# Seven half-size products in both MLPs, values kept in PSUM, and queues ordered by a list scheduler

## The chip, the core and the metric

The kernel runs on one core of one Trainium2 chip. Five engines with queues of their own share it: TensorE (PE, with its weight loads PEld), VectorE (DVE), ScalarE (ACT), GpSimd (POOL) and SyncE (SP, which here issues the DMAs). Each queue runs in order, and an instruction that waits for another engine holds up all that stands behind it on its own queue. The metric is the device time of one launch in microseconds (us).

## The reference

A clustered attention (2 batches, 8 heads, 768 tokens, head size 64) gives 1536 tokens of 512 features. Two MLPs (512 to 2048 to 512) follow, the first with a squared ReLU, the second with a hard swish:

```python
def _moe_ref(x, w_in, w_out):
    h = np.maximum(x @ w_in, 0.0)
    return (h * h @ w_out).astype(np.float32)

def _moe2_ref(x, w_in, w_out):
    h = x @ w_in
    relu6 = np.clip(h + 3.0, 0.0, 6.0)
    g = h * relu6 / 6.0
    return (g @ w_out).astype(np.float32)

x = np.ascontiguousarray(attn_out.transpose(0, 2, 1, 3)).reshape(B * S, H * D)
x = _moe_ref(x=x, **moe_kwargs)
return _moe2_ref(x=x, **moe2_kwargs)
```

The MLP weights are 64-bit floats in memory.

## The kernel before

Every operand of a large product is split into a rounded high part and a low rest, and a product is three matmuls (high by high, high by low, low by high) that add up in PSUM. `decode` (L183 to 219) turns 64-bit weights into such a pair: a clamp on POOL (L193), a scaled copy on ACT (L198), three integer steps on DVE (L203, L205, L209), a rounding on ACT (L213) and a subtraction (L215).

The attention comes first, in an order written out by hand in tables (up to L846). Its last instructions are the rounding and subtraction of the last tiles on POOL (`eh`, `el`), the last product `a` (L709), its sum `u` (L723), the transposes `tn` (L750) and the last quarter of the normalised result, `xh` and `xl` (L756 to L761). The first quarter of the first product of the first MLP (`emit_early`, 48 matmuls of 384 columns) already runs inside it.

The MLPs follow from L850. Both have four stages (`fq`), in each of which 512 of the 2048 hidden features are made and used. A stage has chunks of 512 tokens (384 in the very first stage). `mm1` (L892) makes one chunk's hidden features: four PSUM banks `h`, in each 4 x 3 matmuls (`products`, L229), then `gate` (L237) squares or gates them and splits them into `gh` and `gl`. `mm2` (L912) multiplies a chunk by the second weights into four banks `o`, and each bank is added to `acc` (L941, L943, L947). The loop at L993 calls `mm1` of a chunk and then `mm2` of the chunk before, so that PE has other work while `gate` runs. The order on each queue is the order in which the code calls; only the first steps have their decoding placed by hand (`decoding`, L972). `mm1` and `mm2` of a chunk are 48 matmuls each.

Of the kernel before, what the change touches and what calls it, by code (L numbers as in the profile page):

```python
# [16 lines left out]
I32 = mybir.dt.int32  # L17
# [110 lines left out]
MOST = 2.0**16 * (2 - 2.0**-3 - 2.0**-23)  # L128


@with_exitstack
def cluster_attention_mlp_kernel(
# [718 lines left out]
    with ExitStack() as mctx:  # L851
        t_p = mctx.enter_context(tc.tile_pool(name="t", bufs=2, reuse_waits="tile"))
        acc_p = mctx.enter_context(tc.tile_pool(name="acc", bufs=1, reuse_waits="tile"))
        wr_p = mctx.enter_context(tc.tile_pool(name="wr", bufs=2, reuse_waits="tile"))
        wd_p = mctx.enter_context(tc.tile_pool(name="wd", bufs=2, reuse_waits="tile"))
        w_p = mctx.enter_context(tc.tile_pool(name="w", bufs=3, reuse_waits="tile"))
        g_p = mctx.enter_context(tc.tile_pool(name="g", bufs=2, reuse_waits="tile"))
        g3_p = mctx.enter_context(tc.tile_pool(name="g3", bufs=1, reuse_waits="tile"))
        ps_h = mctx.enter_context(tc.tile_pool(name="ps_h", bufs=4, space=PSUM, reuse_waits="tile"))
        ps_o = mctx.enter_context(tc.tile_pool(name="ps_o", bufs=4, space=PSUM, reuse_waits="tile"))  # L860

        wts = {(0, 0, 0): (w_first[:, 0], w_first[:, 1])}
        idx = [1]

        def load_w(m, fq, which):

            src = w_src(m, fq, which)
            if idx[0] % 4 == 0:
                w = w0_p.tile([P, 2, 4, 512], F32R, tag="w0", name="w0")
# [12 lines left out]
        def run(steps, n=None):
            for _ in range(n) if n else iter(int, 1):
                if next(steps, 0) == 0:
                    break

        acc = acc_p.tile([P, 4, NT], F32, name="acc")

        acc1 = acc.rearrange("p d t -> p (d t)").rearrange("p (b n) -> p b n", n=DM)
        G = {(0, 0, 0): early[0]}  # L890

        def mm1(m, fq, c0, n, between=None):  # L892
            wh, wl = wts[m, fq, 0]
            if (m, fq, c0 + n) == (0, 0, NT):
                gh, gl = (g3_p.tile([P, NF, n], F32R, tag=x, name=x) for x in ("gh3", "gl3"))
            else:
                gh = g_p.tile([P, NF, TC], F32R, tag="gh", name="gh")[:, :, :n]
                gl = g_p.tile([P, NF, TC], F32R, tag="gl", name="gl")[:, :, :n]
            for fb in range(NF):
                h = ps_h.tile([P, TC], F32, tag="h", name="h")[:, :n]  # L900
                for d in range(ND):
                    products(h, wh, wl, fb, d, slice(c0, c0 + n))
                if between:
                    between(0)
                r = t_p.tile([P, TC], F32, tag="r", name="r")[:, :n]
                g = t_p.tile([P, TC], F32, tag="g", name="g")[:, :n]
                gate(m, h, r, g, gh[:, fb], gl[:, fb])
                if between:
# [126 lines left out]
```

## Time and profile before

| | before |
|---|---|
| median of 3 runs | 790.9 us (790.01 to 791.15) |
| span of the profiled execution | 789.0 us |
| PE busy | 771.8 us, 98% of the span |
| DVE, ACT, POOL busy | 547.9, 399.7, 328.5 us |
| granted TensorE clock | full in all 40 slices |
| DMA | 67.27 MB, mean 85 GB/s |

The profiled execution took 789.0 us from its first to its last instruction; the median of the timed runs lies 1.9 us above it. In the page, the busy shares say which engine has no room; the slices say where; the chain of work that ended last says which instructions the end waits for; the groups by shape say what one instruction costs. PE is fully busy in each slice after about 300 us, and the chain there has PE alone.

The matmuls outside the attention, counted in the program's order of the kernel before: 2004 of 512 columns, 336 of 384 and 24 of 256.

### The profile page before, as it was taken

How to read it: one execution, taken by the hardware profiler on the slowest of the kernel's cores; microseconds unless marked ns; L12 is line 12 of the kernel's file. 1: busy time of each engine (PE TensorE's matmuls, PEld its weight loads, DVE VectorE, ACT ScalarE, POOL GpSimd, SP SyncE). 2: the span in 40 equal slices, each digit the busy share in tenths (PEclk: the TensorE clock that was granted, in tenths of full speed). 3: DMA queues.
4: the chain of work that ended last, by engine and by line, in shares of the span. 5: the costliest groups of instructions: out<-in, count | busy, mean ns of one | idle time of the engine just before them, and what ended most of it. 6: DMA issues, size and time to landing. Idle time of an engine off the chain costs nothing.

```text
span 789.0 us, 11571 instructions
## 1 busy us (share of the span) xinstructions
PE 771.8 (98%) x4066; PEld 674.8 (86%) x4066; DVE 547.9 (69%) x891; ACT 399.7 (51%) x803; POOL 328.5 (42%) x440
## 2 busy tenths in 40 slices
PE   7999999999999999999999999999999999999998
PEld 6789999999989899988888888888888888888887
DVE  5889999999998588885654748579465585443332
ACT  4899899899887665554333433424334132111110
POOL 1668778778786562332221313334222121111110
PEclk9999999999999999999999999999999999999999
DMA  8847845836510234441311203022031120000012
GB/s 178 177 106 174 181 94 135 175 89 146 131 34 14 81 97 137 143 145 67 108 50 57 84 24 107 22 86 76 31 107 53 54 81 1 0 1 1 23 46 93
DMA packets 58203, 67.27 MB, mean 85 GB/s; under 512 B 41153, under 2 KB 41409, under 8 KB 58145
## 3 DMA queue, kind: packets, MB, share of 16 engines
q1 hardware_dynamic: 58144, 66.54, 31.7%
q8 instruction: 32, 0.52, 0.3%
q14 instruction: 27, 0.21, 0.1%
HBM read 43.02 MB, written 3.15 MB: 59 GB/s over the span
## 4 chain that ended last, share of the span: by engine, by line
PE 85%; ACT 5%; DVE 5%; issue 2%; POOL 2%; DMA 1%; SPq 0%; ACTq 0%; POOLq 0%
PE o L933 33%; PE h L232 29%; PE a L709 6%; PE t L682 6%; PE s L646 3%; PE s L649 3%; ACT e L666 2%; PE tsim L438 2%; PE tq L393 1%; ACT mt L511 1%; DVE nm L655 1%; ACT eh L692 1%; DVE el L693 1%; ACT et L178 1%; ACT tmp L178 1%
## 5 line engine op out<-in xcount | busy, mean ns | idle before, releaser
L232 PE MATMUL h<-xh,w 128*128 128x512 f32 (+1 forms) x800 | 244.8, 381 | 0.0
L232 PEld LDWEIGHTS h<-xh,w 128*128 128x128 f32 x800 | 149.3, 188 | 26.4 <-DVE xx L756 0.2
L181 POOL TENSOR_SCALAR gh<-g 128x512 fp32r<-128x512 f32 (+1 forms) x96 | 68.9, 718 | 228.1 <-DVE g L243 150.0
L232 PE MATMUL h<-xl,w 128*128 128x512 f32 (+1 forms) x400 | 152.2, 380 | 0.0
L933 PE MATMUL o<-w,gh 128*128 128x512 f32 (+1 forms) x392 | 120.5, 385 | 0.0
L245 DVE TENSOR_TENSOR gl<-g,gh 128x512 fp32r<-128x512 f32 (+1 forms) x96 | 70.4, 736 | 70.4 <-POOL gh L181 70.4
L933 PE MATMUL o<-gh,w 128*128 128x512 f32 (+1 forms) x384 | 114.8, 376 | 0.0
L193 POOL TENSOR_SCALAR t<-wr 128x512 f32<-128x512 f32 (+1 forms) x66 | 56.0, 852 | 113.2 <-DVE w L215 44.5
L682 PE MATMUL t<-ident,e 128*128 128x128 f32 x576 | 93.4, 275 | 8.1 <-ACT e L666 7.4
L242 ACT ACTIVATE r<-h,three 128x512 f32<-128x512 f32 x48 | 32.8, 686 | 120.6 <-PE h L232 120.6
L655 DVE TENSOR_REDUCE nm<-s 128x1 f32<-128x768 f32 x96 | 90.7, 946 | 1.2 <-PE s L649 0.3
L682 PEld LDWEIGHTS t<-ident,e 128*128 128x128 f32 x576 | 70.6, 140 | 20.4 <-ACT e L666 11.4
L666 ACT ACTIVATE e<-s,nm 128x768 f32<-128x768 f32 x96 | 86.3, 899 | 2.1 <-DVE nm L655 1.6
L232 PEld LDWEIGHTS h<-xl,w 128*128 128x128 f32 x400 | 75.1, 188 | 13.0
L933 PEld LDWEIGHTS o<-w,gh 128*128 128x128 f32 x392 | 73.1, 188 | 14.8
L690 POOL TENSOR_TENSOR el<-et,eh 128x384 fp32r<-128x384 f32 x80 | 81.8, 1023 | 6.7
L933 PEld LDWEIGHTS o<-gh,w 128*128 128x128 f32 x384 | 71.4, 188 | 11.6 <-issue 0.4
L198 ACT ACTIVATE u<-t 128x512 f32<-128x512 f32 (+1 forms) x68 | 41.3, 607 | 68.4 <-POOL t L193 67.9
L933 PE MATMUL o<-w,gl 128*128 128x512 f32 (+1 forms) x196 | 75.4, 385 | 0.0
L213 ACT ACTIVATE w<-t 128x512 fp32r<-128x512 f32 (+1 forms) x68 | 39.3, 604 | 69.3 <-PE o L933 41.7
L933 PE MATMUL o<-gl,w 128*128 128x512 f32 (+1 forms) x192 | 72.1, 375 | 0.0
L693 DVE TENSOR_TENSOR el<-t,eh 128x384 fp32r<-128x384 f32 x112 | 61.4, 551 | 14.7 <-ACT eh L692 13.3
(118 smaller groups left out, 1288.2 us busy)
## 6 DMA issues: line engine op xcount, KB each, us to landing
wr<-in_moe_w_out_dram SPq DMA_DIRECT2D x32, 512.0 KB, 3.3
op<-HL SPq DMA_DIRECT2D x84, 192.0 KB, 4.4
wr<-in_moe_w_in_dram SPq DMA_DIRECT2D x28, 512.0 KB, 3.7
rawv<-in_v_dram SPq DMA_DIRECT2D x16, 192.0 KB, 3.6
out_dram<-acc SPq DMA_DIRECT2D x11, 256.0 KB, 2.0
rawq<-in_q_dram SPq DMA_DIRECT2D x14, 192.0 KB, 4.5
rawk<-in_k_dram SPq DMA_DIRECT2D x14, 192.0 KB, 4.0
wr<-in_moe_w_in_dram SPq DMA_DIRECT2D x8, 256.0 KB, 3.0
```

Of the source, the lines that this page charges most:

```text
L181: nc.gpsimd.tensor_scalar(dst, src, 1.0, 0.0, op0=ALU.mult, op1=ALU.add)
L193: (nc.vector if clamp_on_dve or not on_dve and E_CLAMP == "v" else nc.gpsimd).tensor_scalar(t, f(hw), MOST, -MOST, op0=ALU.min, op1=ALU.max)
L198: nc.scalar.activation(u, t, AF.Copy, scale=2.0**-112)
L232: nc.tensor.matmul(h, w[:, d, fs], x[:, d, cs], start=(d == 0 and n == 0), stop=(d == ND - 1 and n == 2),)
L245: nc.vector.tensor_sub(gl, g, f(gh))
L655: nc.vector.tensor_reduce(nm, S_t[n][:, :, :HS], axis=AX.XY, op=ALU.max, negate=True)
L666: nc.scalar.activation(e, s[:, :, :HS], AF.Exp, bias=nm, accum_out=sums[u][:, i * R + r : i * R + r + 1])
L682: nc.tensor.transpose(t[:, c, :], E_t[n][:, half, c * P : (c + 1) * P], ident)
L690: nc.gpsimd.tensor_sub(el, et, f(eh))
L693: nc.vector.tensor_sub(el, t, f(eh))
L709: nc.tensor.matmul(a[:, :HS], vs[:, kr, i, :], x[:, kr, :], start=(kr == 0 and x is eh), stop=(kr == R - 1 and x is el),)
L933: nc.tensor.matmul(o, lhsT, rhs, start=(k == 0), stop=(k == 3 * NF - 1))
```

## The change

The attention is untouched. The MLP part is written anew.

**Seven products.** In six of the eight stages (all but the first of each MLP) the first product is no longer 48 matmuls for a chunk. Two token chunks of 384, two halves of the 512 input features and two halves of 256 hidden features form a 2 x 2 by 2 x 2 block product, and `quad` computes it with seven products of halves and sums of halves instead of eight. A product is 6 matmuls of 384 columns, so a quad is 42 matmuls for four results instead of 48. The sums of weights (`weights_in`: four sums on POOL and five halves split anew) are made in each stage, the sums of tokens (`token_sums`) once for each MLP. Partial results are kept (`keep`, a copy on ACT) and added (`plus`, on DVE, in PSUM).

**Widths.** All first products, and the second products of the first MLP, are now 384 columns wide; the second products of the second MLP stay at 512. Counted in the program's order of the changed kernel: 2112 matmuls of 384 columns outside the attention, 564 of 512 and 24 of 256; the 48 early ones stay.

**PSUM.** The gate writes its product back into the bank it came from, and the rounding (ACT) and the low rest (DVE) read it there. The integer steps of the decoding use a PSUM bank (`low3`) for their intermediate value. The clamp and the scaled copy work in place in the staging tile. POOL no longer rounds the gate's values; it makes the low parts of the weights and half of the token sums.

**Order.** Each instruction of the MLPs is recorded with costs and with what it reads and writes, and `Plan.emit` replays the queues on those costs and calls the instructions in the order that it found; PE's order is given, the other engines take what is ready and due.

Between two quads' products stand the groups of the second product: three inside a quad, thirteen behind it. `hb` are four banks for the first product, `ob` three for the second.

```diff
+class Plan:
+
+    LAG = 0.17
...
+        free = {"POOL": 4.8, "DVE": 2.0, "ACT": 0.5, "DMA": 1.5}
...
+                    end = max(first, o.ready) + o.costs[e]
+                    if not any(
+                        u.ready < end and u.due + shift < end and u.ready + u.costs[e] < end + 0.5
+                        for u in some[:i]
+                    ):
+                        break
...
+        hb, ob, low3 = banks[:4], banks[4:7], banks[7]
...
+        def decoded():
...
+            plan.add({"DMA": 3.0}, lambda: nc.sync.dma_start(to, pieces[n]), (), [rh, rl])
...
+            v, a = t.bitcast(I32), low3.bitcast(I32)
+            pool(0.70, lambda: nc.gpsimd.tensor_scalar(
+                f(hw), f(hw), MOST, -MOST, op0=ALU.min, op1=ALU.max
+            ), [rh], [rh])
+            act(0.63, lambda: nc.scalar.activation(f(hw), f(hw), AF.Copy, scale=2.0**-112), [rh], [rh])
+            dve(0.69, lambda: nc.vector.tensor_scalar(a, hw, 3, None, op0=ALU.logical_shift_left),
+                [rh], ["L"])
...
+        def split(hi, lo, x, hk, lk, k, n, eng="POOL"):
+            act(0.05 + n / 880, lambda: nc.scalar.activation(hi, x, AF.Copy), k, hk)
+            if eng == "POOL":
+                pool(n / 365, lambda: nc.gpsimd.tensor_sub(lo, x, f(hi)), k + hk, lk)
...
+        def weights_in(p, seven):
...
+            half(0, a, x1l)
+            comb(e.tensor_add, d, b, d, x2r, x1r, x2r)
+            comb(e.tensor_sub, b, a, b, x1r, x1l, x1r)
+            half(1, d, x2r)
+            comb(e.tensor_sub, a, d, a, x1l, x2r, x1l)
+            half(3, b, x1r)
+            comb(e.tensor_sub, c, c, a, x2l, x2l, x1l)
+            half(2, a, x1l)
+            half(4, c, x2l)
...
+        T_ENG = ["v", "p"]
+
+        def both(name, o, x, y, ko, kx, ky):
...
+            e, cost = (nc.gpsimd, {"POOL": 1.08}) if eng == "p" else (nc.vector, {"DVE": 0.75})
...
+        def gated(m, i, g):
...
+            if m == 0:
+                act(0.58, lambda: nc.scalar.activation(r, h, AF.Relu), hk, rk)
+                dve(0.56, lambda: nc.vector.tensor_tensor(h, r, h, op=ALU.mult), hk + rk, hk)
...
+            act(0.49, lambda: nc.scalar.activation(gh, h, AF.Copy), hk, ghk)
+            dve(0.56, lambda: nc.vector.tensor_sub(gl, h, f(gh)), hk + ghk, glk)
+
+        def keep(j, i):
+            x, h = xs[j], hb[i][:, :TT]
+            act(0.49, lambda: nc.scalar.activation(x, h, AF.Copy), [("h", i)], [("x", j)])
+
+        def plus(o, i, j):
+            oo, h, x = hb[o][:, :TT], hb[i][:, :TT], xs[j]
+            dve(0.56, lambda: nc.vector.tensor_tensor(oo, h, x, op=ALU.add),
+                [("h", i), ("x", j)], [("h", o)])
...
+        def quad(m, pr, p, seven, group):
...
+            prod(a, w.one[0], w.k(0), x_of(K0, c0), True)
+            keep(0, a)
+            prod(d, w.one[3], w.k(3), t_of(T3[pr]), True)
+            keep(2, d)
+            group()
+            prod(a, w.one[2], w.k(2), t_of(T2[pr]))
+            keep(1, a)
+            prod(b, w.q2[:, :, :, L], w.k(-1), x_of(K1, c0), True)
+            plus(b, b, 0)
+            gated(m, b, slots["11"])
+            group()
+            prod(a, w.one[1], w.k(1), x_of(K0, c1))
+            plus(e, a, 2)
+            gated(m, e, slots["22"])
+            prod(d, w.q2[:, :, :, Rr], w.k(-1), t_of(T4[pr]))
+            plus(d, d, 1)
+            gated(m, d, slots["21"])
+            group()
+            prod(a, w.one[4], w.k(4), x_of(K1, c1))
+            gated(m, a, slots["12"])
...
+        out_order = [(db, fb) for fb in range(NF) for db in range(3)]
+        out_order += [(3, fb) for fb in range(NF)]
...
+                if fq == 0:
+                    act(0.52, lambda: nc.scalar.activation(y, o, AF.Copy), ok, yk)
+                else:
+                    dve(0.57, lambda: nc.vector.tensor_tensor(y, o, y, op=ALU.add), ok + yk, yk)
...
+        first_step(1)
+        later = token_sums(0, 0)
+        for fb in range(NF):
+            weights_out(0, fb)
+        first_step(2)
...
         with tc.manual_schedule():
-            chunks = load_w(0, 0, 1) + load_w(0, 1, 0)
...
+            plan.emit()
```

Three places of the queues follow. The first is POOL at the end of the attention. In the kernel before, `t<-wr` is the clamp of the first weight piece, `g0` the rounding of the early hidden features, `eh` and `el` the last two tiles of the attention:

```order
L690 TENSOR_TENSOR el_3970<-et_3992,eh_3969 128x3x128
L193 TENSOR_SCALAR t_4146<-wr_4144 128x512
L181 TENSOR_SCALAR g0_3716<-rg_4024 128x384
L181 TENSOR_SCALAR eh_3969<-et_4054 128x3x128
L690 TENSOR_TENSOR el_3970<-et_4054,eh_3969 128x3x128
```

The same place of the changed kernel, where `wr0` and `wr1` are the two staging tiles and `acc<-xh,xl` the first token sums, made in the memory of `acc`:

```order
L815 TENSOR_TENSOR el_3970<-et_3992,eh_3969 128x3x128
L1051 TENSOR_SCALAR wr0_4147<-wr0_4147 128x512
L1161 TENSOR_TENSOR acc_4143<-xh_63,xl_64 128x384 x2
L1051 TENSOR_SCALAR wr1_4151<-wr1_4151 128x512
L306 TENSOR_SCALAR g0_3716<-rg_4024 128x384
L1161 TENSOR_TENSOR acc_4143<-xh_63,xl_64 128x384 x2
L306 TENSOR_SCALAR eh_3969<-et_4054 128x3x128
L815 TENSOR_TENSOR el_3970<-et_4054,eh_3969 128x3x128
```

Two token sums and a second clamp have moved ahead of `g0`, and two more sums ahead of the last `eh` and `el`.

The second place is DVE behind the attention's last `xx`, in the first MLP step. Before, the low rests `gl` come between the integer steps of the decoding:

```order
L756 TENSOR_TENSOR xx_4093<-tn_4089,u_3841 128x384
L245 TENSOR_TENSOR gl_4151<-g_4169,gh_4150 128x384
L245 TENSOR_TENSOR gl_4151<-g_4193,gh_4150 128x384
L203 TENSOR_SCALAR u_4177<-u_4177 128x512
L205 SCALAR_TENSOR_TENSOR u_4177<-wr_4174,u_4177 128x512
L209 SCALAR_TENSOR_TENSOR t_4176<-t_4176,u_4177 128x512
L245 TENSOR_TENSOR gl_4151<-g_4216,gh_4150 128x384
```

In the changed kernel `b0` to `b3` are the banks of the first product (a row that writes one is the squaring, the next row that reads it the low rest), and the decoding of two pieces stands ahead of the low rest of `b2`:

```order
L1243 TENSOR_TENSOR w5_4119<-b1_4183,w5_4119 128x384
L1055 TENSOR_SCALAR b7_4207<-wr1_4151 128x512
L1057 SCALAR_TENSOR_TENSOR b7_4207<-wr1_4151,b7_4207 128x512
L1060 SCALAR_TENSOR_TENSOR wt1_4127<-wr1_4151,b7_4207 128x512
L1236 TENSOR_TENSOR b2_4187<-tmp_4115,b2_4187 128x384
L1236 TENSOR_TENSOR b3_4191<-tmp_4115,b3_4191 128x384
L1161 TENSOR_TENSOR acc_4143<-acc_4143 128x384
L1243 TENSOR_TENSOR s1_4159<-b2_4187,s1_4159 128x384
```

What moved: DVE now has the squaring too, and a token sum, between one bank's low rest and the next; PE's next step into `b2` stands behind the last of these rows.

The third place is PE in the first seven-product quad, its last products and the groups of the second product behind them (`b4` to `b6` are the banks `ob`; `x12` is the fourth output block, which uses the bank of the first again):

```order
L1263 MATMUL b2_4187<-gB_4167,w0_68 128x384 x6
L1340 MATMUL b6_4203<-gA_4135,s2_4163 128x384 x3
L1263 MATMUL b0_4179<-xh_63,w0_68 128x384
L1263 MATMUL b0_4179<-xl_64,w0_68 128x384
L1263 MATMUL b0_4179<-xh_63,w0_68 128x384 x2
L1340 MATMUL b4_4195<-gA_4135,s2_4163 128x384 x3
L1340 MATMUL b5_4199<-gA_4135,s2_4163 128x384 x3
L1340 MATMUL b4_4195<-gA_4135,s2_4163 128x384 x12
```

Before, PE wrote a whole bank `o` with 12 matmuls in a row, four banks in turn; now three banks are filled side by side, and the fourth block follows on the first of them two groups later.

## Rows read from the trace of the kernel before

**Rows 1.** The page: span, and busy time, share and instructions of each engine.

```profile
span 789.0 us, 11571 instructions
PE 771.8 (98%) x4066; PEld 674.8 (86%) x4066; DVE 547.9 (69%) x891; ACT 399.7 (51%) x803; POOL 328.5 (42%) x440
```

**Rows 2.** Windows: length, then PE, PEld, DVE, ACT, POOL busy, granted clock, DMA.

```profile
80.00:100.00 20.00, 20.00 (x141) 19.17 (x140) 18.80 (x33) 17.96 (x41) 15.46 (x22) 1.00 0.82 179
...
400.00:420.00 20.00, 20.00 (x90) 16.53 (x90) 14.36 (x22) 9.32 (x16) 7.45 (x8) 1.00 0.26 79
520.00:540.00 20.00, 20.00 (x90) 16.57 (x89) 15.03 (x23) 4.88 (x9) 7.68 (x10) 1.00 0.13 44
```

**Rows 3.** The chain that ended last: start, duration, engine, line, count.

```profile
393.85 10.88 PE o L933 x48
404.73 10.88 PE h L232 x48
```

**Rows 4.** Timeline of PE: every third matmul of 384 columns, start and duration.

```profile
305.76 0.33 PE L933 MATMUL o<-gl,w 128*128 128x384 f32 x1
...
306.28 0.33 PE L933 MATMUL o<-gl,w 128*128 128x384 f32 x1
```

**Rows 5.** Groups by shape: weight loads; busy us and mean ns of one.

```profile
L232 PEld LDWEIGHTS h<-xh,w 128*128 128x128 f32 x800 | 149.3, 188 | 26.4 <-DVE xx L756 0.2
```

**Rows 6.** Groups by shape on DVE: busy us and mean ns of one.

```profile
L693 DVE TENSOR_TENSOR el<-t,eh 128x384 fp32r<-128x384 f32 x112 | 61.4, 551 | 14.7 <-ACT eh L692 13.3 <-POOL eh L181 0.5
...
L209 DVE SCALAR_TENSOR_TENSOR t<-t,u 128x512 int32<-128x512 int32 x60 | 47.7, 795 | 2.7
...
L243 DVE SCALAR_TENSOR_TENSOR g<-r,h 128x512 f32<-128x512 f32 x48 | 32.9, 685 | 32.1 <-ACT r L242 32.1
...
L203 DVE TENSOR_SCALAR u<-u 128x512 int32<-128x512 int32 x60 | 28.8, 485 | 13.3 <-ACT u L198 12.2
...
L245 DVE TENSOR_TENSOR gl<-g,gh 128x384 fp32r<-128x384 f32 x12 | 8.0, 689 | 4.9 <-POOL gh L181 4.9
```

**Rows 7.** Groups by shape on POOL and ACT: busy us and mean ns.

```profile
L690 POOL TENSOR_TENSOR el<-et,eh 128x384 fp32r<-128x384 f32 x80 | 81.8, 1023 | 6.7
...
L692 ACT ACTIVATE eh<-t 128x384 fp32r<-128x384 f32 x112 | 54.8, 491 | 11.8 <-PE t L682 10.3
L193 POOL TENSOR_SCALAR t<-wr 128x512 f32<-128x512 f32 x60 | 53.5, 896 | 112.7 <-DVE w L215 44.5 <-DMA wr<-in_moe_w_out_dram 41.0 <-DMA wr<-in_moe_w_in_dram 22.1
```

**Rows 8.** Timeline of POOL at the attention's end: start, duration, operation.

```profile
262.69 1.01 POOL L690 TENSOR_TENSOR el<-et,eh 128x384 fp32r<-128x384 f32 x1
263.81 0.67 POOL L193 TENSOR_SCALAR t<-wr 128x512 f32<-128x512 f32 x1
...
267.43 0.51 POOL L181 TENSOR_SCALAR eh<-et 128x384 fp32r<-128x384 f32 x1 [0.73 <-ACT et L178]
```

**Rows 9.** Timeline of DVE, PE and ACT there; idle time before in brackets.

```profile
268.26 0.55 DVE L723 TENSOR_TENSOR u<-a,tmp 64x384 f32<-64x384 f32 x1
...
268.96 0.41 PE L709 MATMUL a<-eh,vs 128*128 128x384 f32 x1 [1.15 <-DVE u L723]
...
271.12 0.82 PE L750 MATMUL tn<-ident,rb 128*128 128x128 f32 x6
...
272.48 1.02 DVE L756 TENSOR_TENSOR xx<-tn,u 128x384 f32<-128x384 f32 x2
```

**Rows 10.** Timeline of the weight loads where PE last waited in the MLPs.

```profile
296.54 6.41 PEld L933 LDWEIGHTS o<-g,w 128*128 128x128 f32 x37 [0.45 <-DVE w L215]
...
303.91 0.19 PEld L933 LDWEIGHTS o<-gh,w 128*128 128x128 f32 x1 [0.39 <-issue]
```

**Rows 11.** DMA issues: count, size, median us from issue to landing.

```profile
wr<-in_moe_w_out_dram SPq DMA_DIRECT2D x32, 512.0 KB, 3.3
...
wr<-in_moe_w_in_dram SPq DMA_DIRECT2D x28, 512.0 KB, 3.7
```

More of the change, by code (lines that the diff above doesn't have):

```diff
@@ L851, in cluster_attention_mlp_kernel @@
     with ExitStack() as mctx:
[L852 to L857, printed above, removed]
@@ L882, in run @@
[L882 to L895, printed above, removed]
-            else:
-                gh = g_p.tile([P, NF, TC], F32R, tag="gh", name="gh")[:, :, :n]
-                gl = g_p.tile([P, NF, TC], F32R, tag="gl", name="gl")[:, :, :n]
-            for fb in range(NF):
[L900 to L908, printed above, removed]
-                    between(1)
-            G[m, fq, c0] = (gh, gl)
@@ new lines, in cluster_attention_mlp_kernel, with act, dve, pool @@
+        K0, K1 = slice(0, 2), slice(2, 4)
+        L, Rr = slice(0, P), slice(P, 2 * P)
+        def act(cost, fn, reads, writes):
+            plan.add({"ACT": cost}, fn, reads, writes)
+        def dve(cost, fn, reads, writes):
+            plan.add({"DVE": cost}, fn, reads, writes)
+        def pool(cost, fn, reads, writes):
+            plan.add({"POOL": cost}, fn, reads, writes)
+        def pe(cost, fn, reads, writes):
+            plan.add({"PE": cost}, fn, reads, writes)
+        def cols(c):
+            return slice(c * TT, c * TT + TT)
@@ new lines, in xk, with ak @@
+        def xk(which, ds, c):
+            return [(which, d, c) for d in range(ds.start, ds.stop)]
+        def ak(ds, c):
+            return [k for d in range(ds.start, ds.stop) for k in span("acc", d * NT + c * TT, TT)]
+        pieces = [w_src(0, 0, 1)[:, c] for c in range(4)]
+        for st in range(1, 2 * NS):
+            m, fq = divmod(st, NS)
+            w = (w1_in, w2_in)[m].bitcast(I32).rearrange("(c p) f -> p c f", p=P)
+            for p in range(2):
+                fs = slice(2 * (fq * FQ + 256 * p), 2 * (fq * FQ + 256 * p + 256))
+                pieces += [w[:, 2 * h : 2 * h + 2, fs] for h in range(2)]
+            pieces += [w_src(m, fq, 1)[:, fb] for fb in range(NF)]
@@ new lines, in keep, with product, emit @@
+        def keep(j, i):
[5 more added lines that the diff above has]
+                [("h", i), ("x", j)], [("h", o)])
+        def product(i, terms, keys, first, last=True):
+            h = hb[i][:, :TT]
+            def emit():
+                n = 0
+                for w, x in terms:
+                    for cc in range(2):
+                        for a, b in ((0, 0), (0, 1), (1, 0)):
+                            n += 1
+                            nc.tensor.matmul(
+                                h, w[:, a, cc], x[b][:, cc], start=(first and n == 1),
+                                stop=(n == 6 * len(terms)), skip_group_check=not first,
+                            )
+            hk = [("h", i)]
+            pe(0.173 * 6 * len(terms), emit, keys + ([] if first else hk), hk)
```

546 lines of the change are left out of this document (452 added, 94 removed).

## Prediction

> **What bounds the kernel now.** I read the busy shares first: PE is busy for 771.8 of 789.0 us [rows 1]. The windows then say where: from 400 us on PE is busy for the whole of each window at full clock, DVE for 14.4 and 15.0 us of 20 [rows 2]. The chain confirms it: in the MLPs it is PE alone, 48 matmuls of `mm1` and 48 of `mm2` in turn, 10.88 us each [rows 3], so one matmul of 512 columns takes 10.88 / 48 = 0.2267 us. In that part only fewer or cheaper matmuls shorten the time, and only as long as the other engines still bring their values in time. For 384 columns the starts of every third matmul lie 0.52 us apart [rows 4], 0.1733 us each. A load of weights shows 0.188 us [rows 5], longer than that; it runs beside the matmul ahead of it.
>
> **The matmuls.** Outside the attention there are 2004 of 512 columns, 336 of 384 and 24 of 256. The changed kernel has 564, 2112 and 24. Before: 2004 x 0.2267 + 336 x 0.1733 = 454.3 + 58.2 = 512.5 us. After: 564 x 0.2267 + 2112 x 0.1733 = 127.9 + 366.0 = 493.9 us. That is 18.6 us less. It has two parts. Six stages of four quads save 6 of 48 matmuls each: 24 x 6 x 0.1733 = 25.0 us. Cutting 1440 matmuls of 512 columns into 1920 of 384 gives back 332.7 - 326.4 = 6.3 us, since the narrow one has the greater fixed part. The 256-column ones at the end and the way out after them are the same.
>
> **What must keep pace: DVE.** A turn (one quad and the 16 groups of a second product) has 42 + 48 matmuls of 384 columns, 15.6 us of PE. In it DVE has 3 `plus`, 8 operations of the gate and 4 sums into `acc`, all of 384 columns and with an operand in PSUM, and three integer steps for each of two weight pieces. The nearest rows with a PSUM operand are 0.551 us for 384 columns and 0.685 us for 512 [rows 6]: 15 x 0.551 + 6 x 0.685 = 12.4 us, 79% of the turn. With the rows that have both operands in SBUF, 0.689 and 0.795 us [rows 6], it is 10.3 + 4.8 = 15.1 us, 97%. No row of before shows DVE writing to PSUM, nor two PSUM operands. I take 12.4, because every one of these has a PSUM operand like the first two rows.
>
> The rows show the same subtraction of 384 columns at 0.551 us from PSUM and at 0.689 us with both inputs in SBUF while POOL works. The Trainium skill (SBUF — State Buffer, Who interferes with whom) says that a DVE instruction with two SBUF inputs takes a read port that GpSimd shares, and one with at most one SBUF input outside the two-port modes does not; by it the turn stays at 12.4 us, and against it at up to 15.1. It also has a rule against this change (VectorE: DVE Perf Modes, Why PSUM operands drop a tier): with a PSUM operand an fp32 instruction runs at one element a cycle. The first integer step shows 0.485 us in SBUF and would by that be near 0.685, as I counted it.
>
> **POOL and ACT.** For a stage of four turns (62.4 us) POOL has 8 clamps at 0.896 us and 7680 columns of sums and low parts (16 splits, 8 weight sums) at 1.023 / 384 us each [rows 7]: 7.2 + 20.5 = 27.7 us. ACT has 11 copies and activations a turn at 0.491 us [rows 7], 5.4 us, and the scaled copies and roundings of the weights, 9728 columns a stage, at that row's 0.491 / 384 us each 12.4 us: about 34 us of 62. Both have room. The weights of one set fall free when the third quad ends and are needed one turn and 13 groups later, 15.6 + 6.8 = 22 us, for about 8 us of POOL's work.
>
> **The end of the attention.** Here I walk POOL's queue, because the last tiles of the attention now stand behind MLP work. POOL is free at 262.69 + 1.01 = 263.7 us, and the clamp ends at 264.5 [rows 8]. Now follow two token sums (2 x 1.02), a second clamp (0.67), then `g0` (0.51): 267.7. DVE subtracts `g0` (0.55), makes two `el` (1.1) and the sum `u` (0.55): 269.95, where before `u` ended at 268.81 and PE's last `a` started at 268.96 after a wait of 1.15 us [rows 9]. So `a` starts about 1.1 us later. POOL makes two more sums (2.04) and the last `eh` and `el` (1.53): 271.3, just when the eighth matmul of `a` wants it, 0.1 us more. PE has also two matmuls less ahead of this wait (12 in place of 14), which lengthens the wait by 0.35 and only moves work. PE waits 1.5 us longer than before. Bounds: nothing, if POOL's values are not what PE waits for, and 3 us, if the clamp waits for its DMA.
>
> **The first step.** DVE's `xx` ended at 273.5 [rows 9] and now ends near 274.75. Behind it stand, up to the low rest of `b2`: five gate operations and a low rest of `b2` itself (6 x 0.55, of which overlapping starts take some back), two token sums and a third (3 x 0.6 to 0.69), six integer steps (6 x 0.685), two low rests (1.1): 9 to 11 us, so it ends between 283.7 and 285.8, with ACT's copy of `b2`, which waits behind a weight rounding, at about 284.2. PE comes to its second step into `b2` at 271.12 + 1.25 + 0.57 + 36 x 0.1733 + 24 x 0.1733 = 283.3. It waits 0.9 us there and 0.3 us for `b3`, whose copy on ACT stands behind the scaled copy of a piece whose DMA lands 3.3 to 3.7 us after its issue [rows 11]. Before, PE waited 0.45 and 0.39 us in this stretch [rows 10]. Net +0.4 us; bounds -0.8 and +2.2.
>
> **The turns.** In the first MLP the fourth output block goes into the bank of the first, two groups (1.04 us) after that is full. DVE needs 0.55 us and two handovers, so it must start within about 0.4 us; if one integer step (0.685) has just begun, PE waits up to 0.3 us. There are 16 such places. The other waits in a turn leave more: the low rest that the last group row needs is ready about 0.9 us early when I walk DVE's order with 0.55 us a step. I take 1.5 us in all, between 0 and 16 x 0.3 = 5.
>
> **The sum.** On the profiled execution: 789.0 - 18.6 + 1.5 + 0.4 + 1.5 = 773.8 us. Its own time lies 1.9 us under the median of the runs shown, so I forecast 790.9 - 15.2 = 775.7 us. Low end of the parts: 790.9 - 18.6 - 0.8 = 771.5; high end: 790.9 - 18.6 + 3 + 2.2 + 5 = 782.5.
>
> **Rivals.** (1) *The order is too tight.* The list scheduler counts a clamp at 0.70 us and a transfer at 3.0; the rows say 0.896 [rows 7] and 3.3 to 3.7 [rows 11]. Two pieces a turn are then 0.5 to 0.9 us late each; the scaled copy waits on ACT, and the gate's copies wait behind it. Where a third to a half of that reaches PE, 28 turns lose 0.3 us each, 8.4 us: 784. The same end is reached if DVE pays the SBUF price: 15.1 us at the best share that DVE shows, 18.80 of 20 us in the attention [rows 2], needs 16.1 us, 0.5 us over the turn in 24 turns, 12 us: 788. For it: the queues are in order and nothing slackens them. Against: DVE has a fifth of a turn free and thirteen groups follow each quad.
>
> (2) *DVE becomes the bound.* If an operation that reads and writes PSUM needs a second pass over its columns, the price is the slope of the two PSUM rows, (0.685 - 0.551) / 128 = 1.05 ns a column: 0.40 us for each of seven operations of 384 columns and 0.54 for two of 512, 3.9 us a turn. DVE then needs 16.3, at the share of 0.94 17.3 us, 1.7 over PE's 15.6; 24 turns lose 41 us: 775.7 + 41 - 1.5 = 815, slower than before. It decides from 15.6 + 16.6 / 24 = 16.3 us a turn. Only that no row of before writes PSUM from DVE speaks for it.
>
> (3) *The loads show.* With 0.188 us a load [rows 5] against 0.1733 us a matmul, 1776 more narrow matmuls could lose 0.0147 us each, 26 us: 802. Against: the narrow matmuls of before have a load each too, and stand 0.1733 us apart [rows 4].
>
> That the seven products are not made is no rival: the matmuls are counted in the program's order.
>
> **How the numbers follow.** The forecast has 0.77, rival 1 0.16, rivals 2 and 3 0.04 and 0.02, and 0.01 is left. 0.2% of this kernel, 1.6 us, is about what a measurement can tell from no change: faster means under 789.3, slower over 792.5. Rivals 2 and 3 are slower; of rival 1 0.02 falls within; the rest is faster: 0.92, 0.02 and 0.06. For the range I take 771 to 785: the forecast's own parts and the better half of rival 1.
>
> **What would show it.** Right: PE's groups of 384 columns 0.173 us apart across the quads, PE's idle time in the MLPs under 8 us, DVE's operations with a PSUM result near 0.55 us and its share in a turn near 80%; PE's last `a` waiting 2.5 to 2.8 us, and one wait near 1 us for the low rest of `b2`. Wrong: PE's idle time spread over all turns with DVE as the releaser (DVE over 94%: rival 2; with gaps on DVE, ACT and POOL that end with a DMA or a clamp: rival 1), or narrow matmuls 0.188 us apart with nobody to wait for (rival 3).

## The result and the profile after

| | us | |
|---|---|---|
| before, median | 790.62 | 790.01 to 791.15 |
| changed kernel, median | 780.77 | 780.69 to 780.98 |
| ratio | 0.9875 | 95% interval 0.9861 to 0.9889 |
| forecast | 775.7 | range 771 to 785 |

The kernel is 9.9 us faster; 15.2 were forecast. The profiled execution has a span of 779.2 us. The page's span and busy shares, and windows at the times of [rows 2] (length, then PE, PEld, DVE, ACT, POOL busy, granted clock, DMA):

```profile
span 779.2 us, 12856 instructions
PE 758.9 (97%) x4402; PEld 716.1 (92%) x4402; DVE 595.7 (76%) x1047; ACT 498.8 (64%) x1059; POOL 435.9 (56%) x544
```

```profile
400.00:420.00 20.00, 20.00 (x118) 20.00 (x117) 15.71 (x29) 7.74 (x16) 5.33 (x6) 1.00 0.26 79
520.00:540.00 20.00, 20.00 (x114) 19.59 (x113) 18.48 (x30) 11.64 (x22) 16.26 (x17) 1.00 0.29 89
```

Against [rows 1, 2], PE still bounds it, and DVE has come nearer. PE's waits behind the attention, from the list of its waits (what for, us in all, times, longest):

```profile
PE a L834 <- DVE u L848: 3.2, 1, 3.2
...
PE b L1340 <- ACT acc L1350: 0.4, 1, 0.4
...
PE b L1438 <- DVE s L1243: 0.3, 1, 0.3
PE b L1462 <- ACT acc L1471: 0.3, 1, 0.3
```

All four lie ahead of 316 us; from the first turn at 325.8 us to the end the trace shows no wait of PE over 0.15 us. So the seven products cost no wait, and what is missing must lie ahead of the turns or in the matmuls.

**A common zero.** Executions differ by up to 1.7 us in where the attention ends (its last transposes start at 264.86 us in the trace of before, 265.98 in this one, 264.4 to 266.1 in the others). But for a wait of 0.86 us in e9, the difference arises in the first 35 us, which no kernel here edits, and it goes with the granted clock. In five traces (this one, e12, e11, e2, e6) the clock fell to 0.50 for 3.4 to 6.9 us between 16 and 25 us, and they reach the transposes at 264.9 to 266.1 us; the others reach them at 264.4 to 264.9 (e9 at 265.3). The same window of before and of the changed kernel:

```profile
20.00:30.00 10.00, 8.23 (x56) 6.98 (x55) 8.58 (x18) 8.96 (x20) 7.38 (x10) 1.00 0.67 142
```

```profile
20.00:30.00 10.00, 8.85 (x50) 7.89 (x50) 7.54 (x15) 8.69 (x19) 6.78 (x10) 0.80 0.55 112
```

Whether the change has a part in this, one trace of before can't tell. I therefore count from these transposes. Before has 789.0 - 264.86 = 524.1 us behind them, the changed kernel 779.2 - 265.98 = 513.2: 10.9 us less. All runs, with the stretch from these transposes to the first turn:

| run | median us | behind the transposes | up to the first turn |
|---|---|---|---|
| before | 790.5 to 791.0 | 524.1 | |
| changed | 780.77 | 513.2 | 59.9 |
| changed, again (e12) | 781.01 | 512.9 | 59.6 |
| e1, sums behind the attention | 777.75 | 511.2 | 57.9 |
| e7, filled wait | 779.03 | 512.5 | 59.2 |
| e4, sums after weights | 776.61 | 510.4 | 57.1 |
| e3, eight products | 798.71 | 532.0 | 53.8 |
| e2, output products together | 779.70 | 512.2 | 60.4 |
| e8, more width changes | 782.35 | 516.1 | 61.0 |
| e5, gate in SBUF | 781.34 | 513.8 | 59.6 |
| e9, program order | 792.91 | 525.7 | 70.1 |
| e6, sums and widths | 775.72 | 509.3 | 57.2 |
| e10, hold later | 781.62 | 514.7 | 63.0 |
| e11, hold earlier | 775.63 | 508.7 | 56.9 |

### The profile page after: what moved, and what is told of

Read it like the earlier page. It is cut to its first block, busy times and chain, and to the rows that moved or that the text cites. A ratio compares the mean times of both kernels' runs of the same rounds, so it can differ in the third digit from the quotient of the medians.

```text
span 779.2 us, 12856 instructions
## 1 busy us (share of the span) xinstructions
PE 758.9 (97%) x4402; PEld 716.1 (92%) x4402; DVE 595.7 (76%) x1047; ACT 498.8 (64%) x1059; POOL 435.9 (56%) x544
## 4 chain that ended last, share of the span: by engine, by line
PE 83%; ACT 6%; DVE 6%; DMA 2%; issue 2%; POOL 2%; ACTq 0%; POOLq 0%; SPq 0%; DVEq 0%
PE b L1263 27%; PE b L1379 17%; PE b L1340 15%; PE a L834 7%; PE t L807 6%; PE s L774 3%; PE s L771 3%; ACT e L791 2%; PE tsim L563 2%; PE tq L518 1%; ACT mt L636 1%; DMA op<-HL 1%; DVE acc L1161 1%; ACT eh L817 1%; ACT et L303 1%
## 5 line engine op out<-in xcount | busy, mean ns | idle before, releaser
L1068 POOL TENSOR_TENSOR s<-wt,s 128x512 fp32r<-128x512 f32 (+1 forms) x64 | 66.6, 1051 | 51.3 <-ACT s L1066 42.8
L1263 PE MATMUL b<-xh,w 128*128 128x384 f32 x256 | 74.3, 336 | 0.0
L1263 PE MATMUL b<-xh,s 128*128 128x384 f32 x256 | 74.3, 336 | 0.0
L834 PE MATMUL a<-eh,vs 128*128 128x384 f32 x192 | 70.6, 368 | 3.2 <-DVE u L848 3.2
L306 POOL TENSOR_SCALAR eh<-et 128x384 fp32r<-128x384 f32 x80 | 42.5, 532 | 50.1 <-ACT et L303 47.0
L834 PE MATMUL a<-el,vs 128*128 128x384 f32 x192 | 65.3, 340 | 0.0
L817 ACT ACTIVATE eh<-t 128x384 fp32r<-128x384 f32 x112 | 54.8, 491 | 12.3 <-PE t L807 10.6
L771 PE MATMUL s<-op 128*128 128x384 f32 x192 | 57.5, 382 | 0.0
L1379 PE MATMUL b<-s,gA 128*128 128x512 f32 (+1 forms) x234 | 56.1, 382 | 0.0
L1340 PE MATMUL b<-gA,s 128*128 128x384 f32 x276 | 54.2, 334 | 0.0
L1055 DVE TENSOR_SCALAR b<-wr 128x512 int32<-128x512 int32 x60 | 41.3, 688 | 15.2 <-ACT wr L1054 14.6
```

The source lines that it names most:

```text
L771: nc.tensor.matmul(s[:, h, :HS], o[:, 0, rs], o[:, 2, hs], start=True, stop=False)
L817: nc.scalar.activation(eh, t, AF.Copy)
L834: nc.tensor.matmul(a[:, :HS], vs[:, kr, i, :], x[:, kr, :], start=(kr == 0 and x is eh), stop=(kr == R - 1 and x is el),)
L1068: pool(n / 365, lambda: nc.gpsimd.tensor_sub(lo, x, f(hi)), k + hk, lk)
L1263: nc.tensor.matmul(h, w[:, a, cc], x[b][:, cc], start=(first and n == 1), stop=(n == 6 * len(terms)), skip_group_check=not first,)
L1340: nc.tensor.matmul(o, x[:, ds], y, start=(fb == 0 and k == 0), stop=(fb == NF - 1 and k == 2))
```

## Experiments on the end of the attention

In the changed kernel's trace, POOL, then DVE, then PE there (start, duration, operation, idle time before and its releaser):

```profile
264.90 0.66 POOL L1051 TENSOR_SCALAR wr<-wr 128x512 f32<-128x512 f32 x1
265.53 1.98 POOL L1161 TENSOR_TENSOR acc<-xh,xl 128x384 f32<-128x384 f32 x2
267.47 0.64 POOL L1051 TENSOR_SCALAR wr<-wr 128x512 f32<-128x512 f32 x1
268.19 0.51 POOL L306 TENSOR_SCALAR g<-rg 128x384 fp32r<-128x384 f32 x1
268.67 2.26 POOL L1161 TENSOR_TENSOR acc<-xh,xl 128x384 f32<-128x384 f32 x2
270.90 0.51 POOL L306 TENSOR_SCALAR eh<-et 128x384 fp32r<-128x384 f32 x1
```

```profile
268.74 1.34 DVE L370 TENSOR_TENSOR g<-rg,g 128x384 fp32r<-128x384 f32 x1 [4.27 <-POOL g L306]
270.00 1.01 DVE L818 TENSOR_TENSOR el<-t,eh 128x384 fp32r<-128x384 f32 x2
271.04 0.55 DVE L848 TENSOR_TENSOR u<-a,tmp 64x384 f32<-64x384 f32 x1
```

```profile
271.74 0.41 PE L834 MATMUL a<-eh,vs 128*128 128x384 f32 x1 [3.18 <-DVE u L848]
```

It is the queue that the prediction walked: two sums and a second clamp ahead of `g`, DVE idle for 4.27 us behind it, `a` waiting for `u`. One price was wrong: DVE's subtraction took 1.34 us beside POOL's sums, not 0.55. Behind the wait the granted clock fell to its lower level (1.2 GHz) for a while:

```profile
272.00:274.00 2.00, 2.00 (x11) 2.00 (x11) 0.76 (x2) 0.94 (x2) 0.51 (x1) 0.78 0.00 0
274.00:276.00 2.00, 2.00 (x10) 1.90 (x9) 0.62 (x2) 0.49 (x1) 0.00 (x0) 0.50 0.00 0
```

```profile
273.57 0.52 PE L834 MATMUL a<-el,vs 128*128 128x384 f32 x1
273.89 0.52 PE L834 MATMUL a<-eh,vs 128*128 128x384 f32 x1
```

Matmuls of 384 columns then start 0.32 us apart and not 0.173; these slower starts add up to some 1.7 us.

**e1: the sums behind the attention.**

```diff
                 u1, u2, u3, u4 = part(K0, c1), part(K1, c1), part(K0, c0), part(K1, c0)
+                if n == 0:
+                    late = XH[:, NJ - 1, cols(2)][:, :2]
+                    for e, u in (("DVE", u2), ("POOL", u1)):
+                        eng = nc.vector if e == "DVE" else nc.gpsimd
+                        plan.add({e: 0.1}, lambda eng=eng, u=u: eng.tensor_copy(u[0][:, 0, :2], f(late)),
+                                 [("XH", NJ - 1, 2)], u[1])
```

> Edit: two copies of two columns, one on GpSimd and one on VectorE, read the last normalised piece of the attention and write where the first token sums write; so the first token sums stand behind the attention's end on both engines, and nothing else is moved. Theory (GpSimd ran four of these sums ahead of the last rounding of the gate, VectorE waited 4.27 us for it and could then only slowly free the PSUM bank that the last product of the attention needs; TensorE's 3.18 us wait there took the granted clock down to the 1.2 GHz level for some 3 us, which cost 1.6 us more): the wait falls to at most 0.8 us, the clock stays at its upper level, 780.8 - (2.4 to 3.2) - 1.6 = 776.0 to 776.8 us. Rival A (the sums are not the cause; VectorE would wait for the gate anyway): 780.8 us. Rival B (the wait goes, but the clock falls there for another reason): 777.6 to 778.4 us.

777.75 us (777.38 to 778.38). The wait for `u` is 0.17 us and the clock stays at 1.00: the sums were the cause of the wait. But the time missed the theory's range by 1 us, since later waits grew:

```profile
267.39 0.41 PE L834 MATMUL a<-eh,vs 128*128 128x384 f32 x1 [0.17 <-DVE u L848]
...
281.73 0.45 PE L1444 MATMUL b<-xh,w 128*128 128x384 f32 x1 [0.61 <-DVE s L1249]
...
293.36 3.62 PE L1468 MATMUL b<-g,s 128*128 128x384 f32 x19 [1.58 <-POOL s L1068]
```

POOL now does the sums where it split the output weights `s`. `a` starts 3.1 us earlier behind the transposes; the stretch kept 1.7 to 2.0 of it.

**e7: the wait filled.**

```diff
             if part == 0:
+                if g == 31:
+                    warm_up(ps_t.tile([P, 512], F32, tag="t", name="warm2"), 34)
                 A_t[g] = ps_a.tile([P, 512], F32, tag="a", name="a")
```

> Edit: 34 transposes of the identity matrix into an unused PSUM bank (0.085 us each by the transposes of the trace, 2.9 us together) are put on TensorE ahead of the last product of the attention, so that it works while it would have waited 3.18 us; GpSimd's and VectorE's orders stay as they are. Theory (the drop of the clock behind that wait is the idle time's doing): the product still starts at the same place, but its matmuls and the ones behind it stay at 0.173 us, 780.8 - 1.6 = 779.2 us. Rival (the clock falls there whatever TensorE does, or filling work keeps it no better): 780.8 us, with matmuls 0.32 us apart again.

779.03 us (778.73 to 779.58), the number of the theory, and the clock stayed at 1.00. The trace doesn't bear the reason out. The stretch to the first turn is only 0.4 to 0.6 us shorter; 1.1 us lies ahead of the last transposes, where nothing was edited. The edit also moved 8 of the 12 matmuls of the first step's first block behind `a`. So it doesn't price the clock, and as e12 shows, the clock can stay up there without filling too.

**e12: the changed kernel again**, with no edit.

> No edit: the changed kernel once more, on the chip of these runs. Theory (a wait of 3.2 us ahead of the attention's last product does not always bring the clock down: it fell in three traces with such a wait and stayed up in one): 780.8 us, the wait again 3.2 us, the clock behind it at either level, and runs 1.6 us apart where it differs. Rival (the kernel's wait always brings it down, and the one trace differs for its edit): all runs within 0.5 us and the clock down again.

781.01 us (780.81 to 781.31). The wait is the same and the clock stays up, and the gain is gone at the sixth block of the first step behind the transposes `tn`:

```profile
271.84 0.41 PE L834 MATMUL a<-eh,vs 128*128 128x384 f32 x1 [3.17 <-DVE u L848]
...
286.42 0.44 PE L1438 MATMUL b<-xh,w 128*128 128x384 f32 x1 [1.20 <-DVE s L1243]
```

```profile
272.00:274.00 2.00, 2.00 (x13) 1.96 (x12) 0.85 (x2) 0.93 (x2) 0.59 (x1) 1.00 0.00 0
274.00:276.00 2.00, 2.00 (x15) 2.00 (x14) 1.19 (x3) 0.98 (x2) 0.00 (x0) 1.00 0.00 0
```

In the first trace the same block waited 0.27 us, at 287.00. With the fast clock PE is there 1.5 us earlier and waits 0.9 longer for DVE's `s`, and at ACT's copies later 0.87 in place of 0.38. The two stretches are 59.9 and 59.6 us: here other engines end last behind the lower clock, and it costs next to nothing.

That is not always so. e2 and e8 (below) differ from the changed kernel in the second MLP alone; up to the first turn all queues have the same order, and PE's wait is the same (3.18 and 3.16 us). In e2 the clock was low for some 3.4 us, as in the first trace, in e8 for some 6.8:

```profile
270.00:272.00 2.00, 1.65 (x5) 1.69 (x6) 1.33 (x3) 0.57 (x2) 1.02 (x2) 0.50 0.00 0
...
274.00:276.00 2.00, 2.00 (x10) 1.90 (x10) 0.83 (x2) 0.64 (x2) 0.00 (x0) 0.50 0.00 0
```

Their stretches are 60.4 and 61.0 us. Against e12's 59.6 the lower clock cost 0.2, 0.7 and 1.4 us in these three, one execution each. My theory's fixed price of 1.6 us falls.

**e4: the sums behind the first weight splits too**, by entries in the planner's graph, without an added operation.

```diff
+                hold = G[2, 1][2]
...
-                         xk("XH", ds, c), xk("XL", ds, c))
+                         xk("XH", ds, c) + hold, xk("XL", ds, c))
...
         first_step(1)
-        later = token_sums(0, 0)
         for fb in range(NF):
             weights_out(0, fb)
         first_step(2)
+        later = token_sums(0, 0)
         later()
```

> Edit: in the planner's graph the sums of XH and XL of both token pairs wait for the second gated block of the third token group (no operation is added), and they are entered behind the first output weights; GpSimd so takes the attention's last operations and two of the four weight splits ahead of them. Theory (the earlier experiment took away the 3.2 us wait and the 1.6 us of clock, and gave back 2.5 us because TensorE then waited for a weight split and two gated blocks queued behind the moved sums): with the splits ahead of the sums no wait over 0.5 us between 265 and 320 us is left, and the time is 780.8 - 3.2 - 1.6 - (0 to 0.8) = 775.2 to 776.0 us. Rival (VectorE and GpSimd have too little room between 265 and 320 us, wherever the sums stand there): 777 to 779 us, with waits of 1 us and more for VectorE's or GpSimd's results.

776.61 us (776.22 to 776.95): 0.6 above the theory's range, under the rival's. The stretch is 2.5 to 2.8 us shorter, yet waits of 0.99 us (`s` from POOL) and 1.23 us remain. The second, on PE and on ACT:

```profile
311.27 0.80 PE L1342 MATMUL b<-g,s 128*128 128x384 f32 x3 [1.23 <-ACT acc L1352]
```

```profile
309.66 0.67 ACT L1054 ACTIVATE wr<-wr 128x512 f32<-128x512 f32 x1 [2.02 <-POOL wr L1051]
310.23 0.62 ACT L1066 ACTIVATE w<-wt 128x512 fp32r<-128x512 f32 x1
310.75 1.24 ACT L1352 ACTIVATE acc<-b 128x384 f32<-128x384 f32 x3
```

The copies that free PE's banks stand on ACT behind a scaled weight copy, and that waits 2.02 us for POOL's clamp, itself queued behind sums.

**e10 and e11: the hold moved.** `hold` names the gated block that the sums wait for. These are e6 (below) with `hold = G[2, 3][2]` and with `G[1, 3][2]`:

> Edit: as the kernel with both gains, but the sums wait for the fourth gated block of the third token group, not the second; three of the four weight splits then stand ahead of them on GpSimd. Theory (the sums and the accumulated output share one SBUF tile, so later sums free it later: the 1.0 us wait for a split goes, the 1.2 us wait for the output's first copies grows): 775.7 - 1.0 + (1 to 3) = 775.7 to 777.7 us. Rival (only the split's wait moves): 774.7 us.

> Edit: as the kernel with both gains, but the sums wait for the fourth gated block of the second token group, some 5 us earlier. Theory (earlier sums free the accumulated output's tile earlier, but stand ahead of more weight splits): the 1.2 us wait for the output's first copies falls to 0.4, the 1.0 us wait for a split grows to 1.6 as with the sums right behind the attention: 775.5 us, within 0.5. Rival (the two stretches do not share the sums): 774.5 or 776.5 us.

e10: 781.62 us (781.12 to 782.37). Theory and rival both missed it; all waits behind `a` grew: 1.70 us for DVE's `s`, 1.21 for POOL's, 1.75 and 1.55 for ACT's copies. Behind the waits of 1.21 and 1.75 us the clock fell as well (0.55 and 0.60 in the windows from 296 to 300 us). e11: 775.63 us (775.26 to 776.59). The two waits moved as the theory said, POOL's `s` from 0.99 to 1.88 and ACT's copy from 1.23 to 0.71; the time agrees too, but can't be told from e6's 775.72. My reason for e10, a shared SBUF tile, was not shown; the rows of e4 show queue order on ACT and POOL instead. At each of the five places tried between 265 and 320 us the sums push something else there.

## Experiments on the products

**e3: eight products throughout.**

```diff
-            seven = fq > 0
+            seven = False
...
-        later = token_sums(0, 0)
```

(The other calls of `token_sums` go as well.)

> Edit: every stage takes the eight products of halves that so far only the first stage of the second MLP takes; the token sums and the sums of weight quarters are then not made at all. All else (values kept in PSUM, widths, the list scheduler) stays. Theory (a turn's matmuls bound everything behind the attention): 24 turns x 6 x 0.1733 = 25.0 us more than the kernel with the token sums behind the attention, since here no token sums stand at the attention's end either: 776.4 + 25.0 = 801.4 us. Rival A (part of the seven products' gain was already lost to waits or to loading weights): 780.8 + (15 to 20) less the 4.4 of the attention's end = 791 to 797 us. Rival B (the attention's end is not the token sums' doing): 780.8 + 25.0 = 805.8 us.

798.71 us (798.61 to 799.02), 2.7 under the theory's 801.4 and over rival A's 797. The trace says where that is. All 24 turns are 1.04 us longer (15.60 to 16.64 in the first MLP), which is 25.0 us and the whole term. Without the sums PE has one wait left behind the transposes, though:

```profile
267.82 0.41 PE L834 MATMUL a<-eh,vs 128*128 128x384 f32 x1 [0.47 <-DVE u L848]
```

and the stretch is 53.8 us, not 59.9. Behind the transposes e3 needs 18.9 to 19.1 us more than the changed kernel: 25.0 less the 5.9 to 6.1 that the sums of tokens and weights cost there. e1 still has some of that cost, so the difference to it is 21.0 and not 25.0. This is the price of the change that I undersized.

**e2 and e8: fewer and more changes of width.** In the second MLP a turn took 15.63 us (mean of 11), not the 42 x 0.1733 + 36 x 0.2267 = 15.44 of the prediction's prices; in the first it was 15.60, as worked out. Three 512-column matmuls between narrow ones take 0.70 us from start to start, not 0.68:

```profile
531.85 0.86 PE L1379 MATMUL b<-s,s 128*128 128x512 f32 x3
532.55 0.33 PE L1263 MATMUL b<-xh,s 128*128 128x384 f32 x1
```

```diff
-                quad(m, pr, p, seven, lambda: next(some)())
+                quad(m, pr, p, seven, (lambda: None) if m else lambda: next(some)())
+                run(some)
```

> Edit: in the second MLP the three groups of 512-column matmuls that stand between the 384-column products of a turn go behind them, so that a turn changes between the two widths 2 times and not 8. Theory (a turn of the second MLP takes 15.63 us and not the 15.44 worked out because a change of the width costs about 0.024 us): turns of 15.49 us, 15 to 16 turns x 6 x 0.024 = 2.2 us less, 778.6 us. Rival A (the 0.19 us per turn come from the 512-column groups themselves, wherever they stand): 780.8 us. Rival B (without the groups between them, the products wait for the copies and sums of their PSUM banks, up to 0.3 us at three places of a turn): 780.8 to 792 us, with waits of TensorE in the trace from 560 us on.

In e8 `group` is also called after the first, third and fifth of the seven products, six groups in all:

```diff
             keep(0, a)
+            more()
             prod(d, w.one[3], w.k(3), t_of(T3[pr]), True)
```

> Edit: in the second MLP three more groups of 512-column matmuls are moved in between the 384-column products of each turn of seven, so that such a turn changes between the widths 14 times and not 8. Theory (with the groups together a turn lost 6 changes and 0.09 us, 0.015 us per change): turns of 15.63 + 0.09 = 15.72 us, 12 turns, 1.1 us more in all, 781.9 us. Rival (the turns became shorter there since waits went, not changes): turns of 15.63 us, 780.8 us.

The first matmul of two successive turns in the changed kernel, e2 and e8:

```profile
611.02 0.33 PE L1263 MATMUL b<-xh,w 128*128 128x384 f32 x1
...
626.62 0.33 PE L1263 MATMUL b<-xh,s 128*128 128x384 f32 x1
```

```profile
609.97 0.33 PE L1263 MATMUL b<-xh,w 128*128 128x384 f32 x1
...
625.52 0.33 PE L1263 MATMUL b<-xh,s 128*128 128x384 f32 x1
```

```profile
611.06 0.33 PE L1263 MATMUL b<-xh,w 128*128 128x384 f32 x1
...
626.78 0.33 PE L1263 MATMUL b<-xh,s 128*128 128x384 f32 x1
```

That is 15.60, 15.55 and 15.72; the means of 11 turns are 15.63, 15.54 and 15.78. No turn of the three has a wait of PE. Six changes fewer give 0.09 us and six more cost 0.15. So alternation costs, as the theory has it, but at 0.015 to 0.025 us a change and not one price; with two changes a turn is still 0.10 over its sum. The starts within a turn, averaged over the 11 turns, say where this is: in the changed kernel they lie off their price only in the first three to nine matmuls behind a change (0.02 to 0.04 us in all), and within 0.002 us of it elsewhere. In e2, 0.02 us also stand in the last narrow matmuls ahead of a change. e2's 779.70 us (778.94 to 779.86) is 1.1 to 1.3 under the changed kernel, the 15 x 0.09 of its turns, where 2.2 was expected. e8's 782.35 us is 0.5 over its theory. Its runs spread from 780.45 us at a mean granted clock of 0.999 to 784.12 at 0.993, and of the 2.9 us that its trace is longer than the changed kernel's behind the transposes, 1.2 lie ahead of the first turn. Its turns, 1.7 us longer in all, are the evidence, not its time.

**e5: the gated value in SBUF.**

```diff
-                    h, r, 6.0, h, op0=ALU.min, op1=ALU.mult
-                ), hk + rk, hk)
+                    r, r, 6.0, h, op0=ALU.min, op1=ALU.mult
+                ), hk + rk, rk)
...
-            dve(0.56, lambda: nc.vector.tensor_sub(gl, h, f(gh)), hk + ghk, glk)
+            dve(0.80, lambda: nc.vector.tensor_sub(gl, r, f(gh)), rk + ghk, glk)
```

> Edit: the gated value of a hidden block is written to an SBUF tile and not back to its PSUM bank, and VectorE's subtraction for its low part reads SBUF twice (795 ns for one in the trace before, 557 ns from PSUM in the trace after). Nothing else. Theory (VectorE is busy for some 12 of the 15.6 us of a turn and TensorE never waits for it; 4 x 0.24 = 0.95 us more per turn make 13 of 15.6): 780.8 us, within 0.5. Rival (the planner's order leaves no room for longer VectorE operations, as the prediction's first rival had it): 784 to 788 us, with waits of TensorE for VectorE in the turns.

781.34 us (780.01 to 781.62), 0.3 to 0.6 over the changed kernel. The subtraction went from 551 to 762 ns:

```profile
L1243 DVE TENSOR_TENSOR gA<-b,gA 128x384 fp32r<-128x384 f32 x60 | 32.0, 551 | 1.7 <-ACT gA L1242 1.5
```

```profile
L1243 DVE TENSOR_TENSOR gA<-tmp,gA 128x384 fp32r<-128x384 f32 x60 | 45.4, 762 | 4.8 <-ACT gA L1242 3.1
```

Two early turns of the first MLP became 0.53 and 0.32 us longer, 25 stayed as they were. So the theory nearly holds (it had no turn longer), and the rival's 784 is far off.

**e9: program order in place of due times.**

```diff
+        for o in ops:
+            o.due = o.n * 1e-6 - 1e6
         free = {"POOL": 4.8, "DVE": 2.0, "ACT": 0.5, "DMA": 1.5}
```

> Edit: the planner's due times are replaced by the number under which an operation was entered; operations are still taken when they are ready, but among ready ones the first entered goes first, not the one that is due first. Theory (the order costs nothing only because the due times let the gates of a turn go ahead of the next turn's weights): the weights, entered ahead of the turn that they follow, now go first on VectorE, ScalarE and GpSimd, a gated block comes up to 2 us late at each turn's first out product, 28 turns x 0.3 to 1 us = 789 to 809 us. Rival (with 76% of VectorE and 64% of ScalarE busy any order of ready operations does): 780.8 to 783 us.

792.91 us (792.55 to 793.37), 12 over the changed kernel. That is in the theory's range, but not for its reason: two turns are longer, by 1.8 and 0.6 us. The rest is the stretch ahead, 70.1 us, where PE waits for the weight splits of ACT and POOL:

```profile
293.83 0.62 PE L1464 MATMUL b<-g,s 128*128 128x384 f32 x2 [3.11 <-ACT s L1068]
...
303.97 1.99 PE L1464 MATMUL b<-g,s 128*128 128x384 f32 x9 [1.19 <-POOL s L1070]
307.03 3.58 PE L1464 MATMUL b<-g,s 128*128 128x384 f32 x19 [1.08 <-POOL s L1070]
```

The granted clock was low there too (0.50 in the windows from 296 to 302 us), which I can't part from the waits. The due times are worth most in the stretch where the sums stand, and little in the turns.

**e6: both gains**, the edits of e4 and e2.

> Edit: the sums as in the kernel with the sums after the weights, and in the second MLP the 512-column groups of a turn together. Theory (the two gains lie in different stretches and add up; the turns of the second MLP went from 15.63 to 15.54 us when the groups stood together, 15 x 0.09 = 1.35 us): 775.6 - 1.35 = 774.2 us. Rival (the second change only moved waits): as the kernel with the sums after the weights, 775.6 us.

775.72 us (774.84 to 776.32; ratio 0.9812, interval 0.9799 to 0.9826). This is the rival's number, but only because e4 measured 776.61 us and not the 775.6 that both forecasts started from. The second edit added 0.9 to 1.1 us to e4's gain, under the 1.35 expected (one turn had 15.86). With e11 this is the fastest here, some 5 us under the changed kernel.

## Why the prediction was right, and where it was off

The direction and the range held; the point was 5 us low. By its steps:

1. **The matmuls, -18.6: held.** e3 gives the 25.0 us of the six matmuls a quad back in its turns; the 6.3 us of narrower cutting fit it: e3 lies 532.0 - 524.1 = 7.9 us over before, which is 6.3, and 2.9 for the widths (item 6), less about 1.3 that PE lost by waiting in before (1.15 us at `a`, about 0.6 behind it) and not in e3 (0.47).
2. **DVE, 12.4 us a turn: held.** 11.5 to 12.6 us in the first four turns. The window of the second and two groups of DVE's operations (busy us and mean ns of one):

```profile
341.44:357.05 15.61, 15.61 (x92) 15.61 (x91) 11.76 (x22) 8.21 (x17) 6.11 (x7) 1.00 0.22 68
```

```profile
L1055 DVE TENSOR_SCALAR b<-wr 128x512 int32<-128x512 int32 x60 | 41.3, 688 | 15.2 <-ACT wr L1054 14.6
L1251 DVE TENSOR_TENSOR b<-b,tmp 128x384 f32<-128x384 f32 x72 | 40.8, 566 | 68.0 <-PE b L1263 36.4 <-ACT wr L1054 29.7 <-ACT w L1066 1.5
```

   The two unseen forms cost nothing new: from and to PSUM 0.566 us at 384 columns, 0.688 for the integer step. Rivals 2 and 3 fall: PE waits in no turn, and narrow matmuls stay 0.173 us apart. The rules of the Trainium skill that the prediction weighed agree. The first integer step went from 0.485 us [rows 6] to 0.688 on PSUM (VectorE: DVE Perf Modes, Why PSUM operands drop a tier). Operations with two SBUF inputs slowed down beside POOL, and those with one in PSUM didn't (SBUF — State Buffer, Who interferes with whom); the last section has the rows.
3. **The end of the attention, +1.5: right in mechanism, near in size.** The wait was 3.18 us where 2.5 to 2.8 was said, mostly by the subtraction of 1.34 us. Against the 1.15 of before that is +2.0. (`a` starts 5.76 us behind the last transposes, 4.10 before, only +1.7, since two matmuls less stand ahead of it.)
4. **The first step, +0.4: the term that failed.** The sums cost 5.9 to 6.1 us up to the first turn (e3), 2.7 of it at `a`; so 3.2 to 3.4 us are lost behind it. Before lost about 0.6 there: the 0.84 of [rows 10] is idle time of the weight loads, and PE's own starts slipped by 0.4 and 0.2. The first of the two, eight matmuls that would take 1.54 us without it:

```profile
295.73 1.96 PE L933 MATMUL o<-g,w 128*128 128x384 f32 x8
```

   So the term is +2.6 to +2.8, over my upper bound of 2.2. In e12 the loss is waits alone: 1.20 us for the low rest of `b2`, the wait near 1 us that the prediction named, then 0.26 and 0.87 for ACT's copies of the output blocks, each with slower starts behind it. In the first trace about half of it is the lower clock, for which I had no term, and the wait for `b2` is 0.27 us. I walked two blocks, `b2` and `b3`; I left out ACT's copies, and sized DVE's sums at 0.6 to 0.69 where the first two took 1.28 and 1.04.
5. **The turns, +1.5: no wait at all**, the low bound; the fourth output block was in time at all 16 places. Rival 1 falls by time; POOL's clamps took 0.68 us on average, not 0.896. Its mechanism, late clamps that hold up ACT, is real, but in the stretch ahead of the turns (e4).
6. **Not priced: alternating widths**, 0.19 us over the sum in each of 15 turns: +2.9.

With these: -18.6 + 2.0 + 2.7 + 2.9 = -11.0 us, against -10.9 and -11.2 from the last transposes on in the two traces. So these terms leave nothing larger than the traces' own difference. The 1.1 us by which both profiled executions of the changed kernel reach these transposes later than that of before go with the lower clock of their first 25 us; they make the rest of the way to the measured 9.9. Part of the forecast's closeness is luck: the 1.5 us of the turns, which did not come, hide half of the 2.9 for the widths, which I had not priced.

## What to carry to other kernels

Work that is moved ahead to feed a cheaper steady state has to be done somewhere: sum what each engine must do in the stretch where it lands, and walk every in-order queue that PE later waits for, not the first two. A price from runs of equal matmuls is a little low where widths alternate. And a slow clock or a wait costs only what the next releaser doesn't absorb, here 0.2 to 1.4 us for one stretch: look who ends last behind it before pricing it.

## What the runs showed of the hardware

- A TensorE wait of 3.16 to 3.70 us behind full work was followed by the lower clock (0.50 granted) in four traces (the first of the changed kernel, e2, e8, e9) and not in two (e5, e12). In e10 it fell behind waits of 1.21 and 1.75 us. I did not expect that either outcome occurs, nor that its price in the same order of queues is 0.2 to 1.4 us.
- In five of the fourteen traces the clock also fell between 16 and 25 us, for 3.4 to 6.9 us, in a part of the program that no kernel here edits.
- Matmuls of 384 and 512 columns in turn cost 0.015 to 0.025 us per change with no wait shown; in the changed kernel the loss stands in the first three to nine matmuls behind a change.
- From 265 us on, DVE's sums and subtractions of two SBUF tiles (128x384) took 0.54 to 1.65 us: 1.27 each in the row below beside POOL's sums, 0.55 with POOL idle. With one input in PSUM they kept to 0.54 to 0.57. On POOL and DVE of the changed kernel (POOL was idle from 309.4 to 312.05 us):

```profile
304.51 2.62 POOL L1161 TENSOR_TENSOR g<-acc,g 128x384 fp32r<-128x384 f32 x2
```

```profile
303.71 2.54 DVE L1161 TENSOR_TENSOR gB<-acc,gB 128x384 fp32r<-128x384 f32 x2
...
310.34 0.55 DVE L1161 TENSOR_TENSOR acc<-acc 128x384 f32<-128x384 f32 x1
```
